# Attention value products in 64x64 TensorE tiles, with keys split over the partition halves and new instruction orders

## The chip, the cores and the metric

The kernel runs on one core of a Trainium2 chip. A core has five engines that each work through a queue of their own: TensorE (PE; its weight loads are listed as PEld), VectorE (DVE), ScalarE (ACT), GpSimd (POOL) and SyncE (SP), which here only starts transfers. Sixteen DMA engines serve them all. The metric is device time in microseconds (us).

## The reference

Windowed attention with sink keys, then a gated feed-forward network with an RMS norm in front. Four batches, eight heads, 768 positions, head size 64; window 128, four sinks; model width 512, hidden width 1536.

```python
scores = scale * np.matmul(q, k.transpose(0, 1, 3, 2))
keep = (pos[None, :] < n_sink) | ((rel >= 0) & (rel < window))      # rel = query - key
a = softmax(np.where(keep, scores, -1e9))
x = np.matmul(a, v)                          # heads side by side: 3072 x 512
xn = x / rms(x) * rms_g
g = xn @ w_gate
out = (silu(g) * (xn @ w_val)) @ w_out
```

## The kernel before

The 3072 rows are 24 blocks of 128 positions, g = 0 to 23; block g is block t = g mod 6 of batch g div 6. In the text "t=0" is a batch's first block, "last" is t=5.

For each block, q and k come from HBM as bf16 by GpSimd's queue (`load_bf16`, L351; `load_v`, L355). They are turned so that the head dimension lies on partitions: by TensorE and a copy for blocks 0 to 7 (`pe_t`, `copy_t`), by a DMA transpose on SP's queue from block 8 (`dma_t`, L457). The *scores* of a block are its 128 keys against the queries of its own and of the next block, since a window of 128 reaches from a key into the next block and no further. They are laid out with keys on partitions, so that after the exponential on ScalarE and a mask the tile e can be the stationary operand of the *value product* (`av`, L602): for each head, e of the block before (its second half) and e of the block itself, times v with a column of ones, which gives the row sums. From t=2 the four sink keys, which are then outside the window, are scored apart (`sink_s`, L739) and added to the product by one matmul for four heads (L606), u = 0 for heads 0 to 3 and u = 1 for heads 4 to 7. For nine of the blocks this sink matmul is instead issued with the next block's scores, in smaller tiles (`sink_av`, L633, "hosted").

From block 4 the scores of t=1 to 4 leave out quarters that the mask makes zero: `tri_scores` (L551) uses TensorE as four tiles of 64x64, row half by head parity, column half by key half, with matmuls of 192, 64 and 128 columns. t=0 and last blocks use 64x128 tiles (`scores` L474, `scores_last` L492), sinks 128x32. The value product uses the full 128x128 array throughout. The mask is a VectorE multiplication up to block 15 (`tri_mask` L578, `mask_dve` L542, `mask_dve_last`); from block 16 most masks are GpSimd selects (`tri_pool` L590, `mask_pool_last` L524).

VectorE then divides by the row sums (`normal`, L655), ScalarE sums the squares (`square`), VectorE works out the norm and scales (`rms`, L674), and x is transposed again (`pe_x`, `dma_x`).

The network works on six groups G of four blocks. For a hidden chunk TensorE makes g and v (L975), ScalarE the tanh (L982), VectorE two products (`silu` L986, `hidden` L993); `project` (L1004) multiplies by w_out, ScalarE evacuates, SP stores. Group 0 is done in quarters of its columns, groups 1 and 2 in halves (`CHUNKS`), so that they can begin before all four blocks are there.

Nothing decides the order while the program runs. Each piece of work is registered with `plan.op` and gets a number; `ORDER` (L70) lists the numbers for each engine, `TURNS` interleaves the engines' lists into one program order and `BANKS` names the PSUM bank that each piece takes. The nanoseconds and priorities in the `op` calls play no part in the result; only the lists do. Each engine runs its list strictly in order. Semaphores that follow from the tiles make it wait.

## Time and profile before

Three runs took 241.34, 241.84 and 242.26 us, median 241.84. The profiled execution spans 241.9 us from its first to its last instruction; the profile gives no other time for it. The granted TensorE clock is 1.00 throughout.

| stretch, us | PE busy | DVE busy | ACT busy | POOL busy |
|---|---|---|---|---|
| 30 to 62 | 31.16 of 32 | 28.37 | 21.96 | 23.49 |
| 62 to 71 | 6.89 of 9 | 8.10 | 6.58 | 3.08 |
| 71 to 100 | 28.79 of 29 | 26.84 | 15.94 | 13.61 |
| 100 to 140 | 39.69 of 40 | 36.74 | 22.55 | 9.80 |
| 140 to 180 | 39.41 of 40 | 31.70 | 20.02 | 14.65 |
| 180 to 239 | 58.66 of 59 | 33.31 | 18.01 | 0.14 |

How to read the profile: a digit in a row of slices is the busy share of one fortieth of the span, in tenths. A line of the timeline is a run of like instructions: start, length to the end of the last one, engine, line, operation, names, and the tile (rows x columns of the array) with the operand's size. The end of a matmul is modelled and takes in the drain of the array, so a following matmul starts before it; what a matmul costs is the distance to the next start. In lists of waits, "A <- B: total, times, longest" is idle time of A that ended when B did.

### The profile page before, as it was taken

Reading aid. Unit: us, or ns where it says so; the run is one execution under the profiler, and the core shown is the slowest. Engines: PE = TensorE matmul, PEld = TensorE weight load, DVE = VectorE, ACT = ScalarE, POOL = GpSimd, SP = SyncE. Lnnn points to the kernel's source line nnn. Section 1 sums busy time; section 2 is a strip of 40 time slices with the busy share of each in tenths; the row PEclk is TensorE's granted clock in tenths of the full one; section 3 lists DMA queues with packets and bytes.
Section 4 is the critical chain, followed back from the end, with each engine's and each line's share of the span. In section 5 each row is a group of like instructions: output and inputs, shape, how many; then the busy total and the mean of one; then the engine's idle time right before and its main releaser. Section 6 shows DMA issues by size and latency. Waiting matters only on the chain.

```text
span 241.9 us, 5897 instructions
## 1 busy us (share of the span) xinstructions
PE 231.3 (96%) x2329; PEld 147.6 (61%) x2354; DVE 187.4 (77%) x478; ACT 122.8 (51%) x267; POOL 89.2 (37%) x116
## 2 busy tenths in 40 slices
PE   7889999999879999999999999999999999999995
PEld 5568986876668776777876644445554444444443
DVE  3599989989979999999898989994569946537520
ACT  4776368667766574337654464454543321233112
POOL 8985894597526554000004982022540000000000
PEclk9999999999999999999999999999999999999999
DMA  9999999999999999999601999527010114101024
GB/s 128 143 183 195 182 178 194 162 143 139 137 151 152 138 143 154 132 233 156 126 2 24 119 150 123 131 70 128 3 23 0 32 36 173 43 0 47 0 87 173
DMA packets 113741, 27.42 MB, mean 113 GB/s; under 512 B 103857, under 2 KB 110769, under 8 KB 113714
## 3 DMA queue, kind: packets, MB, share of 16 engines
q0 software_dynamic: 81760, 13.90, 79.3%
q1 hardware_dynamic: 31810, 12.95, 29.8%
q8 instruction: 18, 0.29, 0.5%
q10 hardware_dynamic: 144, 0.20, 0.2%
q14 instruction: 9, 0.07, 0.1%
HBM read 28.35 MB, written 6.29 MB: 143 GB/s over the span
## 4 chain that ended last, share of the span: by engine, by line
PE 67%; DMA 20%; POOL 6%; issue 2%; DVE 2%; SPq 2%; POOLq 0%
PE v L975 20%; PE o L1008 20%; PE g L975 18%; DMA wo<-in_moe_w_out_dram 5%; DMA qkT<-q 4%; DMA wv<-in_moe_w_val_dram 4%; DMA wg<-in_moe_w_gate_dram 3%; DMA q<-in_q_dram 3%; POOL v L357 2%; SPq L459 2%; PE s L563 2%; PE av L621 2%; POOL k L353 1%; PE av L616 1%; PE o_last L1028 1%
## 5 line engine op out<-in xcount | busy, mean ns | idle before, releaser
L975 PE MATMUL v<-xnt,wv 128*128 128x128 bf16 (+2 forms) x527 | 72.2, 282 | 0.4 <-DMA wv<-in_moe_w_val_dram 0.2
L975 PE MATMUL g<-xnt,wg 128*128 128x128 bf16 (+2 forms) x521 | 71.3, 281 | 0.4
L1008 PE MATMUL o<-wo,hT 128*128 128x512 bf16 x259 | 65.3, 379 | 1.1 <-issue 0.5
L982 ACT ACTIVATE th<-g 128x512 bf16<-128x512 f32 x72 | 41.7, 599 | 48.4 <-PE g L975 48.2
L988 DVE SCALAR_TENSOR_TENSOR p<-th,g 128x512 bf16<-128x512 bf16 x72 | 48.1, 682 | 18.9 <-ACT th L982 18.7
L975 PEld LDWEIGHTS <-wv 128*128 128x128 bf16 x528 | 43.3, 98 | 21.3 <-DMA wv<-in_moe_w_val_dram 0.6
L998 DVE TENSOR_TENSOR hT<-p,v 128x512 bf16<-128x512 bf16 x72 | 48.1, 682 | 9.3 <-PE v L975 7.8
L975 PEld LDWEIGHTS <-wg 128*128 128x128 bf16 x528 | 42.8, 98 | 19.3 <-issue 1.0
L1008 PEld LDWEIGHTS <-hT 128*128 128x128 bf16 x276 | 25.4, 98 | 26.5 <-issue 0.2
L597 POOL TENSOR_SCALAR_AFFINE_SELECT e<-e 128x512 bf16<-128x512 bf16 x20 | 12.7, 656 | 54.4 <-ACT e L572 53.0
L572 ACT ACTIVATE e<-s 128x384 bf16<-128x384 f32 x52 | 23.1, 495 | 12.5 <-PE s L563 12.5
L1016 ACT ACTIVATE osb<-o 128x512 f32<-128x512 f32 x23 | 13.4, 597 | 21.8 <-PE o L1008 18.0
L357 POOL DMA_DIRECT2D v<-in_v_dram x24 | 21.3, 888 | 8.5 <-DMA q<-in_q_dram 3.8
L353 POOL DMA_DIRECT2D q<-in_q_dram x23 | 20.4, 891 | 9.9 <-DMA k<-in_k_dram 6.7
L353 POOL DMA_DIRECT2D k<-in_k_dram x23 | 20.4, 889 | 9.1 <-DMA v<-in_v_dram 4.5
L669 ACT ACTIVATE sq<-x 128x512 bf16<-128x512 bf16 x24 | 15.1, 631 | 14.8 <-DVE x L661 14.5
L661 DVE TENSOR_TENSOR x<-av,rden 128x256 bf16<-128x256 f32 x48 | 20.4, 424 | 1.7
L693 DVE SCALAR_TENSOR_TENSOR xr<-x,r,gb 128x512 bf16<-128x512 bf16 x24 | 18.7, 778 | 0.8
L621 PE MATMUL av<-v,e 128*128 128x65 bf16 x192 | 16.4, 193 | 0.3 <-DMA v<-in_v_dram 0.3
L536 ACT ACTIVATE e<-s 128x512 bf16<-128x512 f32 (+1 forms) x36 | 15.1, 519 | 1.6 <-PE s L485 1.5
L616 PE MATMUL av<-v,e 128*128 128x65 bf16 x160 | 14.8, 193 | 0.0
L621 PEld LDWEIGHTS <-e 128*128 128x128 bf16 x192 | 12.7, 97 | 2.8 <-DVE e L547 0.4
(78 smaller groups left out, 192.6 us busy)
## 6 DMA issues: line engine op xcount, KB each, us to landing
out_dram<-osb SPq DMA_DIRECT2D x23, 256.0 KB, 2.2
v<-in_v_dram POOLq DMA_DIRECT2D x24, 128.0 KB, 8.9
q<-in_q_dram POOLq DMA_DIRECT2D x23, 128.0 KB, 8.1
k<-in_k_dram POOLq DMA_DIRECT2D x23, 128.0 KB, 9.6
wo<-in_moe_w_out_dram POOLq DMA_DIRECT2D x2, 768.0 KB, 11.3
wg<-in_moe_w_gate_dram POOLq DMA_DIRECT2D x5, 256.0 KB, 8.0
wv<-in_moe_w_val_dram POOLq DMA_DIRECT2D x5, 256.0 KB, 8.9
stage<-in_k_dram SPq DMA_DIRECT2D x1, 256.0 KB, 3.0
```

The source lines that it names most:

```text
L353: nc.gpsimd.dma_start(out=T[name, g], in_=block_of(src, g))
L357: nc.gpsimd.dma_start(out=V16[b][:, t, :, 0:D], in_=block_of(v, g))
L572: nc.scalar.activation(out=e_tile(g)[:, x:x + 2, 0:TW], in_=BANK.pop(("s", g, u, hi))[:, 0:2 * TW].rearrange("p (j c) -> p j c", c=TW), fu ...
L616: nc.tensor.matmul(out=dest, lhsT=T["e", g - 1][:, x, P:2 * P], rhs=V16[b][:, t - 1, h, :], start=(t == 1), stop=False, skip_group_check=True,
L621: nc.tensor.matmul(out=dest, lhsT=T["e", g][:, x, 0:P], rhs=V16[b][:, t, h, :], start=(t == 0), stop=True, skip_group_check=True,)
L661: nc.vector.tensor_tensor(out=T["x16", g][:, 4 * u:4 * u + 4, :], in0=pvv[:, :, 0:D], in1=rden.unsqueeze(2).to_broadcast((P, 4, D)), op=AL ...
L693: nc.vector.scalar_tensor_tensor(out=T["xr", g], in0=T.pop(("x16", g)).rearrange("p h d -> p (h d)"), scalar=r[:, 3:4], in1=gb, op0=ALU.mu ...
L975: nc.tensor.matmul(out=ps[:, i * n:(i + 1) * n], lhsT=w_sb[:, kt, ft * P:(ft + 1) * P], rhs=T["xnt", G][:, kt, cols], start=(kt == 0), sto ...
L982: nc.scalar.activation(out=T["th", key], in_=BANK[("g", key)], func=ACT.Tanh, scale=0.5,)
L988: nc.vector.scalar_tensor_tensor(out=T["p1", key], in0=T.pop(("th", key)), scalar=1.0, in1=BANK.pop(("g", key)), op0=ALU.add, op1=ALU.mult,)
L998: nc.vector.tensor_tensor(out=T[hk][:, i:i + n, cols], in0=T.pop(("p1", key)).rearrange("p (n c) -> p n c", n=n), in1=BANK.pop(("v", key)) ...
L1008: nc.tensor.matmul(out=BANK[("o", G, tb)], lhsT=T["h", G, ft // 4][:, ft % 4, tb * P:(tb + 1) * P], rhs=wo[:, ft, :], start=(ft == 0), sto ...
```

## The change

From block 4 every block is "packed". Heads 0 to 3 keep their keys in partitions 0 to 63 of the score tiles and heads 4 to 7 in 64 to 127; the two halves of a block's keys lie side by side in columns. So scores and product both run as four 64x64 tiles: in the scores the row half is the head parity and the column half is u; in the product the row half is u and the column half is the half of the queries. The product issues 64x64 matmuls of 65 columns, round by round over the four tiles, and leaves out the quarters that are zero: each tile's queue has 4 or 8 matmuls for t=0, 12 or 16 for t=1 and 12 for t≥2, after the sinks, which are no longer hosted. Scores are 16 matmuls for every block. Block 4 still reads block 3's e in the old layout, so its product is partly full-array ("mixed").

For a key half that lies in the other partitions than its heads, v must move: `move_v` copies 64 partitions x 4 heads x 65 columns twice a block, on VectorE for blocks 4, 6, 7, 8, 10, 14, 15, 16, 20, 21 and 23, on ScalarE for the other nine. The mask is now one VectorE multiplication over the columns that need it (two for t=0) against a new constant `corner`, which eight VectorE instructions make; GpSimd makes no masks any more. Loads of late blocks no longer wait for scores ten blocks earlier (`LOAD_LEAD`), gates between scores and the network (`gate_of`) and the merged scores of blocks 17 and 18 are gone, and each load buffer has its own tag.

All lists are new. Read by what the numbers stand for, TensorE's list around blocks 4 to 9 (`+sa` is a hosted sink matmul, g/v/o are pieces of the network, numbered by group and place):

```
before: s4  ss  o o  pe_t k5  o  pe_x3  s5  av4  g  av4  g  pe_t q6  g  pe_t q7  o  v  av5  o  av5
        pe_t k6  v v  pe_t k7  s6  o  pe_x4  o  s7  o  pe_x5  av6  o  av6  g  o  g  av7 av7  o o v
        pe_x6  g  s8  ss  g v g  s9+sa8  v v  pe_x7  av8 av8 ...
after:  s4  ss  o o  pe_t k5  pe_t k6  o  pe_x3  AV4 s5  g  pe_t q6  pe_t q7  g g  AV5  v o v o  s6
        o  pe_x4  o o o  pe_t k7  pe_x5  v g v g  AV6 s7  v g o g  AV7 s8  o g  pe_x6  o v g
        ss  s9  v v  pe_x7  o v  AV8 AV9 ...
```

Further on, products and scores stand side by side as s11 AV10, AV11 s12, AV12 AV13, s16 AV14, AV15 AV16 s17, AV17 s18, AV18 AV19, s22 AV20, s23 AV21, AV22 AV23. GpSimd's list of loads:

```
before: ... q6  wo 0-6  k5  v4  wo 6-12  q7  v8  q8  v5  k6  k7  k8  v6  v7  q9  k9  v9  q10  k10  v10 ...
after:  ... q6  wo 0-6  k5  k6  v4  v5  q7  wo 6-12  q9  q8  q10  k8  k7  v6  v9  v7  k9  k10  q11  k11  v8 ...
```

SP's transposes begin q8, q9, k8, k9, q10, (store), q11, k10, k11 before, and q8, q10, q9, k8, k9, (store), k10, q11, k11 after; later x 8 and x 9 stand ahead of k13, and q18 ahead of x 12, x 14 and x 13.

The core of the diff (lists, bank names and removed functions left out; the removed ones are in the listing above):

```diff
+    def make_corner():
+        nc.vector.memset(corner, 1.0)
+        nc.vector.memset(corner[:, 3], 0.0)
+        for i in range(2):
+            r = slice(i * DH, (i + 1) * DH)
+            nc.vector.tensor_copy(out=corner[r, 0:3:2], in_=masks[r, 1, :, r])
+            nc.vector.tensor_copy(out=corner[r, 4:7:2], in_=masks[r, 1, :, r])
+        for i in range(2):
+            nc.vector.memset(corner[i * DH:i * DH + NS, 0:4], 1.0)
...
-            needs = [("s", g - LOAD_LEAD)] if g >= LEAD_FROM else []
+            needs = []
...
+    def width(g):
+        t = g % NT
+        return 4 * DH + TW if t == 0 else 2 * TW if t + 1 < NT else TW
+
+    def piece(g, kh):
+        t = g % NT
+        if t == 0:
+            return (kh, 4 - kh, 4 * kh)
+        return (kh, 3, 3 * kh) if t + 1 < NT else (kh, 2 - kh, 2 * kh)
...
+    def packed_scores(g):
...
+        for j in range(2):
+            for kh in range(2):
+                q0, n, c = piece(g, kh)
+                q0, n, c = t * P + q0 * DH, n * DH, c * DH
+                for u in range(2):
+                    for hi in range(2):
+                        pr, hp = slice(hi * D, (hi + 1) * D), 2 * u + j
+                        k0 = t * P + kh * DH
+                        slot, o = (("s", g, hi, j), c) if t + 1 < NT else (("s", g, hi, 0), j * w + c)
+                        nc.tensor.matmul(
+                            out=BANK[slot][u * DH:(u + 1) * DH, o:o + n],
+                            lhsT=qkT[pr, 1, hp, k0:k0 + DH], rhs=qkT[pr, 0, hp, q0:q0 + n],
+                            start=True, stop=True, tile_position=(hi * D, u * DH),
+                            skip_group_check=True,
+                        )
...
+    def packed_mask(g):
+        t, w = g % NT, width(g)
+        if t == 0:
+            for i in range(2):
+                ev = packed_e(g)[:, 2 * i * w:2 * (i + 1) * w].rearrange("p (x c) -> p x c", c=w)
+                m = corner.rearrange("p n c -> p (n c)").unsqueeze(1).to_broadcast((P, 2, w))
+                nc.vector.tensor_tensor(out=ev, in0=ev, in1=m, op=ALU.mult)
+            return
+        ev = packed_e(g).rearrange("p (x n c) -> p x n c", c=DH, n=3)[:, :, 0:3:2, :]
+        m = corner[:, 4:7:2] if t + 1 < NT else corner[:, 4:5].to_broadcast((P, 2, DH))
+        m = m.unsqueeze(1).to_broadcast((P, ev.shape[1], 2, DH))
+        nc.vector.tensor_tensor(out=ev, in0=ev, in1=m, op=ALU.mult)
+
+    def move_v(g, copy):
+        b, t = divmod(g, NT)
+        vx = T["vx", g] = vxpool.tile([P, 4, VW], BF16, name="vx")
+        for u in range(2):
+            here, there = (slice(x * DH, (x + 1) * DH) for x in (u, 1 - u))
+            copy(out=vx[here], in_=V16[b][there, t, 4 * u:4 * u + 4, :])
+
+    def packed_av(g):
...
+        queues = {}
+        for u in range(2):
+            for c in range(2):
+                own = [(0, kh) for kh in range(1 + c)]
+                old = [(1, kh) for kh in range(2) if t == 1 or kh >= c] if t and not mixed else []
+                queues[u, c] = [
+                    (j, hi, *x, x == (own + old)[0], x == (own + old)[-1])
+                    for j in range(2) for hi in range(2) for x in own + old
+                ]
+        for i in range(max(map(len, queues.values()))):
+            for (u, c), queue in queues.items():
+                if i >= len(queue):
+                    continue
+                j, hi, old, kh, first, final = queue[i]
+                k, h, rows = g - old, 2 * j + hi, slice(u * DH, (u + 1) * DH)
+                q0, n, col = piece(k, kh)
+                col = (2 * hi + j) * width(k) + (col + c + 2 * old - q0) * DH
+                vk = V16[b][rows, t - old, 4 * u + h, :] if kh == u else T["vx", k][rows, h, :]
+                nc.tensor.matmul(
+                    out=BANK["av", g, u][c * DH:(c + 1) * DH, h * VW:(h + 1) * VW],
+                    lhsT=T["e", k][rows, col:col + DH], rhs=vk, start=first and t < 2,
+                    stop=final, tile_position=(u * DH, c * DH), skip_group_check=True,
+                )
...
         if g >= PACK_FROM:
             packed_block(g)
         else:
             block_scores(g)
```

## The prediction, written before the result was known

> **What bounds the kernel now.** I read the page's busy shares and slices first, then TensorE's waits from 30 to 239 us, then single groups in the timeline.

> ```profile
> PE 231.3 (96%) x2329; PEld 147.6 (61%) x2354; DVE 187.4 (77%) x478; ACT 122.8 (51%) x267; POOL 89.2 (37%) x116
> ...
> PE   7889999999879999999999999999999999999995
> ...
> DVE  3599989989979999999898989994569946537520
> ```

> TensorE is full from slice 4 to the end; VectorE is full beside it until about 140 us. TensorE's waits from 30 us on:

> ```profile
> PE s L563 <- DMA qkT<-q: 1.3, 1, 1.3
> PE s L563 <- DMA qkT<-k: 0.8, 1, 0.8
> ...
> PE av L621 <- DMA v<-in_v_dram: 0.3, 1, 0.3
> ```

> There are three real ones: v of block 5 at 48.4 us (0.32), kT of block 8 at 64.6 us (0.78), qT of block 10 at 69 us (1.32), 2.4 us together. Everything else is work in the list's order, so a TensorE nanosecond saved or added after 30 us is one at the end, as long as no new wait opens. The chain shows where the longest wait comes from:

> ```profile
> 47.27 7.30 DMA q<-in_q_dram
> 54.59 1.20 SPq L459
> ...
> 59.75 10.61 DMA qkT<-q
> ...
> 70.49 0.54 PE s L563 x16
> ```

> A late load on POOL's queue, then SP's transposes one by one, then 10.6 us for one to land while loads crowd the DMA engines.

> **TensorE's work.** The groups to price it by (start, length, count; lengths end with the modelled drain, so I count from start to next start):

> ```profile
> 91.19 0.20 PE L616 MATMUL av<-v,e 128*128 128x65 bf16 x1
> 91.22 0.19 PE L621 MATMUL av<-v,e 128*128 128x65 bf16 x1
> 91.25 0.38 PE L1008 MATMUL o<-wo,hT 128*128 128x512 bf16 x1
> ...
> 75.38 0.54 PE L563 MATMUL s<-qkT 64*64 64x192 bf16 x24
> 75.74 0.30 PE L641 MATMUL av<-vsk,esk 64*64 64x260 bf16 x4
> 75.97 0.50 PE L975 MATMUL g<-xnt,wg 128*128 128x256 bf16 x3
> ```

> A full-array value matmul takes 0.030 us. The 24 score matmuls in 64x64 tiles carry 3,072 columns and take 0.36 us: 768 columns in each of four tiles, at the 2.4 columns per ns that 512 columns in 0.216 us give, are 0.32. So four tiles do run beside each other. Read by single starts, a group that follows one of another array shape begins 0.096 us later than the columns before it explain (0.095 to 0.099 at some 25 places, both ways): that is a **change of shape**.

> *Value product.* Before, a block with t≥1 has 16 matmuls, 16 x 0.030 = 0.48 us, and with t≥2 its sinks: two full-array ones of 0.11 where they are in the product (48.27 to 48.38), 0.135 as four tiles (75.74 to 75.97 less a change), 0.11 as two 64x128. After, a tile's queue holds 8 matmuls (t=0), 16 at most (t=1) or 12 (t≥2, the zero quarters gone). Inside a score group a 64-column matmul is followed on its own tile, with a weight load between, after 0.028 us (75.500 to 75.528). I take 0.028 for a round: 0.22, 0.45, and 12 x 0.028 + 0.135 = 0.47. Saved: six blocks with four-tile sinks (8, 9, 14, 15, 20, 21) 6 x 0.145 = 0.87; three with two-tile sinks (10, 11, 22) 0.36; four with sinks in the product (5, 16, 17, 23) 4 x 0.23 = 0.92; t=1 three times 0.03; t=0 and the mixed block 4 nothing. **2.2 us.**

> *Scores.* t=0: 2,048 columns in two tiles (0.43) become 896 per tile (0.385), three times; last blocks 0.22 become 0.17, four times; the others keep 768 per tile. **0.35 us.**

> *Changes of shape.* A product that stands alone now costs two. The new list puts most beside scores or each other (product 4 with scores 5, 6 with 7, 8 with 9, 15 with 16 and scores 17, 22 with 23). Counted through both lists from the scores of block 4, 44 changes become 55: 11 x 0.096 = **1.06 us** back.

> Net **-1.5 us**. Bounds for the new rounds: below, bare columns, 65 / 2.4 = 0.027; above, issue. A t≥2 product is 104 instructions in 0.47 us, 4.5 ns each; the densest stretch of before is 48 in 0.32 us, 6.7 ns each, but that one was bound by its columns, and its first eight instructions came in 0.012 us. At 6.7 ns a product takes 0.70. I take 0.028, the row nearest in kind.

> [...]

> **VectorE and ScalarE.** By start to next start: a mask of 1,024 columns is 0.60 (L547), the triangular one 0.66 + 0.45 = 1.11, one of 512 0.335. Blocks from 4 on before: 8 x 1.11 + 4 x 0.335 + 6 x 0.60 = 13.8, and 24 GpSimd selects (15.2 us) for the late blocks. After, all on VectorE: 13 x 0.60 + 4 x 0.335 + 3 x 1.15 (two of 896) = 12.6. New: the eleven value moves on VectorE, two copies of 64x260 each, between 0.18 (64x16) and 0.335 (128x512): I take 0.22, 4.8 us; the corner masks, eight small operations, about 1.3; one transpose copy more from ScalarE each for q and x, 0.7. VectorE +5.6 us of 180, ScalarE nine moves of about 0.7, +6. What hides it: TensorE is behind neither in its own sums. Adding durations in the order of the lists, the work that VectorE owes before each value product ends, against TensorE's sum at that product, 5.0 us early at the tightest before (blocks 6 and 7) and 4.5 to 5.0 early after (blocks 5 and 7), 8 and more from block 12 on. VectorE runs about 4.4 us further behind its sum than TensorE (block 5's last rms operation ends at 55.5 us with 42.2 summed; TensorE is at 57.9 with 49.0), so the cover early on is a few tenths. If it is gone, the excess of the first 100 us, some 2 us, comes through.

> **Loads and SP's queue.** In POOL's list q9 and q10 stand directly behind wo and v8 goes far back; v5 and k6 go ahead of q7. Loads land in order, about 1 us apart by then, so I read times off the places: v5 43.4 us (48.9 before), q9 48.9 (54.6), q10 50.5 (57.3). SP's list has q10 ahead of q9 and the k: the transposes that scores 8 and 9 wait for go out 2 to 8 us earlier. All three old waits go: **-2.4 us**. Late next: k6, whose transposition now follows k5's on TensorE with a landing near 41.5 us (0.3 to 0.5 us wait); v4 with its move ahead of product 4 (0.3); the masks of block 3, pushed back by the corner masks and a later score group (0.4). **+1.2 us.** Late loads lose their gates and the selects ahead of them (k20 went out at 133.3 us, 38 us after q20), so they crowd transposes at 100 to 120 us; those have 4 us and more in hand, so nothing there. On SP the transpose of k13 now stands behind those of x 8 and 9, and several behind the one of q18, which waits for a later load; by the same reading all are 4 to 10 us ahead of their scores. Queued behind the new waits: behind k6's transposition everything on TensorE; behind v4's move, on VectorE, a hidden product and block 4's normalisation; behind v5's move, on ScalarE, block 5's exponentials, which TensorE asks for only 3 us later.

> **Sum.** The profiled span is 241.9 us and the median 241.84, so the sum can stand on the median: 241.84 - 1.5 - 2.4 + 1.2 = **239.1 us**.

> **Rivals.**
> 1. *The tiles starve* (slower). If instructions come at 6.7 ns, a t≥2 product costs 0.23 more (13 times), t=1 0.30 and t=0 0.10 (three each): +4.2, 243.3. [...] It decides from about 0.64 us per t≥2 product. For it: 48 different weight loads in a row of 65-column matmuls occur nowhere before. Against it: the 28 ns, and eight instructions in 12 ns. Chance 0.27, of it a third for the rule.
> 2. *The cover goes* (no gain). VectorE's extra work and the pairs, which make product 8 wait for block 9's readiness, open waits of about 2.5 us beyond mine, and all is given back: 241.6. For: the few tenths of cover at 40 to 60 us. Against: the margins after. Chance 0.15.
> 3. *Forecast*, 238.2 to 240.6, chance 0.58. Its lower end is no new wait at all; its upper end, old transposes still late by a microsecond and a half.

> Less than 0.5% (1.2 us) I couldn't tell from no change here. Range 238.2 to 244.0: the forecast, rival 2 and the larger part of rival 1. Faster: 0.58 x 0.87 + 0.27 x 0.03 + 0.15 x 0.2 = 0.54; slower: 0.01 + 0.27 x 0.67 + 0.15 x 0.3 = 0.24; same 0.22.

> **What would show it.** The value product of block 9 or 16, start to next start: 0.47 right, 0.64 or more rival 1. Changes still 0.096, between 64x64 groups of scores and products none. TensorE's waits on qkT near 65 and 70 us gone; small ones at 41 to 44 us. Rival 2 would show as TensorE waiting for masks, moves or rms between 40 and 80 us. Most likely to make me wrong is a round longer than 28 ns, then a transpose that SP holds behind a later load.

## The result, and the profile after it

The changed kernel takes **244.41 us** (median of five, 243.56 to 245.23), the kernel before beside it 242.17 (241.34 to 242.59): ratio **1.0095**, 95% interval 1.007 to 1.0121. It is slower by some 2.2 us; I had forecast 239.1 us and no case of mine gave both this time and its cause. The profiled execution took 244.64 us with a span of 242.9 us.

The first lines of its page, against those shown of before:

```profile
PE 232.3 (96%) x2893; PEld 147.6 (61%) x2920; DVE 191.1 (79%) x507; ACT 127.4 (52%) x283; POOL 74.3 (31%) x92
...
PE   7899999969999999999999999999999999999995
...
DVE  2499989759999999998999989996879975543810
PEclk9799999999999999999999999999999999999999
```

TensorE has 566 weight loads more (2920 against 2354), is as busy as before, and has one slice, the ninth (48.6 to 54.6 us), in which it is idle for a third. VectorE has 3.7 us more work. (The 7 in the clock's row, a stretch at half clock from 9.3 to 12.7 us, is not of the change: e1 below has none.) What TensorE waited for from 30 us on (engine, line, waited for: us in total, times, longest):

```profile
PE v L941 <- issue: 1.8, 1, 1.8
PE o L974 <- issue: 0.8, 5, 0.2
PE v L941 <- DVE hT L964: 0.4, 1, 0.4
PE s L488 <- DVE p L954: 0.3, 1, 0.3
PE av L612 <- DVE hT L964: 0.3, 1, 0.3
```

The old waits for `qkT` (1.3 and 0.8) and for v (0.3) are gone, as forecast. (The line of `o`, 0.8 us in five places, is no wait: there the record of the first of a group's four matmuls is missing, with its 0.216 us, while all four weight loads are in the trace.) In their place stands one wait of 1.8 us for "issue", that is for nothing that the profile shows. The timeline has it in the middle of a v product (start, length, count, idle time before):

```profile
48.51 0.61 PE L941 MATMUL v<-xnt,wv 128*128 128x128 bf16 x8
50.93 0.44 PE L941 MATMUL v<-xnt,wv 128*128 128x128 bf16 x5 [1.81 <-issue]
```

The matmul that waited reads the same input as the eight ahead of it, and its weights had long landed: the last load of `wv` went out at 23.4 us, and none took more than 9.9. From the last start (48.90) to the next (50.93) are 2.03 us where 0.06 are usual: a **standstill of 1.97 us**. What the chip did meanwhile is on a DMA queue. Of all DMA queues in the window 48.0 to 49.5 us:

```profile
q0 software_dynamic: 1759, 0.22, 232.9%
q8 instruction: 1, 0.02, 4.3%
```

One packet on q8, the instruction queue: 16 KB, from 48.33 to 49.37 us, between 1,759 packets of loads. TensorE goes on 1.56 us after its end. Over the whole span the queue has 23 packets in the changed kernel and 18 in the one before:

```profile
q8 instruction: 23, 0.38, 0.6%
```

My **theory A**: TensorE's instructions come in these packets of 16 KB, a block of 256 in each. The trace's rows have 5,866 instructions of TensorE in the changed kernel and 4,736 in the one before, 255 for each of the 23 packets and 263 for each of the 18. The packet at 48.33 us started 4.0 us after the block ahead of it had been begun (44.3). By the theory a packet queues behind the loads, and TensorE stands still when 256 instructions are used up sooner than the next packet comes. Between 44.3 and 48.9 us the changed kernel uses 256 instructions in 4.6 us; the kernel before used its block from there on in 8.6 us. **Rival B**: the loss is VectorE's and ScalarE's, the cover of my rival 2, through the corner masks and the copies of v.

To tell them apart I counted TensorE's instructions up to each standstill, from the trace's rows in order: weight loads, one matmul for each of them (27 of the changed kernel's matmul records are missing) and semaphore instructions. If A holds, all stand at one remainder modulo 256, wherever the boundary is pushed, and each ends the same time after a packet.

### The profile page after: what moved, and what is told of

Same layout as the page of the kernel before. It is cut to its first block, busy times and chain, and to the rows that moved or that the text cites. A ratio compares the mean times of both kernels' runs of the same rounds, so it can differ in the third digit from the quotient of the medians.

```text
span 242.9 us, 7031 instructions
## 1 busy us (share of the span) xinstructions
PE 232.3 (96%) x2893; PEld 147.6 (61%) x2920; DVE 191.1 (79%) x507; ACT 127.4 (52%) x283; POOL 74.3 (31%) x92
## 4 chain that ended last, share of the span: by engine, by line
PE 66%; DVE 24%; issue 4%; ACT 3%; DMA 2%; SPq 0%; DVEq 0%; ACTq 0%
PE o L974 21%; PE g L941 17%; PE v L941 17%; DVE p L954 5%; DVE hT L964 5%; PE s L548 3%; DVE r L702 2%; PE av L635 2%; DVE xr L706 2%; DVE x L674 2%; DMA stage<-in_q_dram 2%; DVE vx L587 1%; PE o_last L994 1%; DVE e L580 1%; DVE e L516 1%
## 5 line engine op out<-in xcount | busy, mean ns | idle before, releaser
L941 PE MATMUL v<-xnt,wv 128*128 128x128 bf16 (+2 forms) x521 | 71.4, 281 | 2.5 <-issue 1.8
L974 PE MATMUL o<-wo,hT 128*128 128x512 bf16 x257 | 63.7, 379 | 1.7 <-issue 0.8
L954 DVE SCALAR_TENSOR_TENSOR p<-th,g 128x512 bf16<-128x512 bf16 x72 | 47.9, 683 | 13.9 <-ACT th L948 13.6
L941 PEld LDWEIGHTS <-wg 128*128 128x128 bf16 x528 | 43.4, 98 | 21.9 <-issue 0.5
L964 DVE TENSOR_TENSOR hT<-p,v 128x512 bf16<-128x512 bf16 x72 | 47.7, 683 | 10.3 <-PE v L941 7.9
L564 ACT ACTIVATE e<-s 128x384 bf16<-128x384 f32 (+1 forms) x72 | 32.1, 503 | 13.9 <-PE s L548 11.9
L706 DVE SCALAR_TENSOR_TENSOR xr<-x,r,gb 128x512 bf16<-128x512 bf16 x24 | 18.1, 752 | 0.8
L673 DVE RECIPROCAL rden<-av 128x4 f32<-128x4 f32 x48 | 8.4, 176 | 4.3 <-PE av L635 2.3
L580 DVE TENSOR_TENSOR e<-e,corner 128x1024 bf16<-128x1024 bf16 (+1 forms) x17 | 10.5, 625 | 1.5 <-ACT e L564 1.4
L635 PEld LDWEIGHTS <-e 64*64 64x64 bf16 x888 | 10.2, 106 | 1.6 <-DVE p L954 0.4
L635 PE MATMUL av<-v,e 64*64 64x65 bf16 x444 | 11.1, 193 | 0.0
L702 DVE TENSOR_SCALAR r<-r 128x1 f32<-128x1 f32 x48 | 10.0, 209 | 0.9
```

Source lines behind the costliest of these rows:

```text
L564: nc.scalar.activation(out=packed_e(g)[:, x * w:(x + n) * w], in_=BANK.pop(slot)[:, 0:n * w], func=ACT.Exp, scale=inv_sqrt_d,)
L635: nc.tensor.matmul(out=BANK["av", g, u][c * DH:(c + 1) * DH, h * VW:(h + 1) * VW], lhsT=T["e", k][rows, col:col + DH], rhs=vk, start=first ...
L706: nc.vector.scalar_tensor_tensor(out=T["xr", g], in0=T.pop(("x16", g)).rearrange("p h d -> p (h d)"), scalar=r[:, 3:4], in1=gb, op0=ALU.mu ...
L941: nc.tensor.matmul(out=ps[:, i * n:(i + 1) * n], lhsT=w_sb[:, kt, ft * P:(ft + 1) * P], rhs=T["xnt", G][:, kt, cols], start=(kt == 0), sto ...
L954: nc.vector.scalar_tensor_tensor(out=T["p1", key], in0=T.pop(("th", key)), scalar=1.0, in1=BANK.pop(("g", key)), op0=ALU.add, op1=ALU.mult,)
L964: nc.vector.tensor_tensor(out=T[hk][:, i:i + n, cols], in0=T.pop(("p1", key)).rearrange("p (n c) -> p n c", n=n), in1=BANK.pop(("v", key)) ...
```

## The experiments

All runs at once; "standstills" are those of the run's own profile between 30 and 135 us, start to next start less the usual step. The time is the median of 4 to 12 executions (e5: one), the ratio is to the kernel before on the same chip.

| run | edit to the changed kernel | standstills, us | us | ratio to before |
|---|---|---|---|---|
| after | none | 1.97 | 244.41 | 1.0095 |
| e1_same | none | 1.83 + 0.23 | 244.03 | 1.0079 (1.0055 to 1.0104) |
| e2_phase150 | 150 more warm-up instructions | 1.57 + 2.14 | 246.24 | 1.0178 (1.0155 to 1.0200) |
| e3_phase74 | 74 more | 0.39 + 1.82 + 0.26 + 0.76 | 245.49 | 1.0147 (1.0120 to 1.0174) |
| e4_corner | corner masks early | 1.76 + 0.35 | 244.26 | 1.0101 (1.0066 to 1.0137) |
| e5_before | the kernel before | none | 242.74 | |
| e6_nomove | no copies of v | 1.67 + 0.2 + 0.85 | 243.38 | 1.0058 (1.0040 to 1.0076) |
| e7_clear | 208 + 32 more | 0.88 + 0.76 | 244.20 | 1.0101 (1.0085 to 1.0117) |
| e8_clearcorner | e7 and e4 | 0.95 + 0.98 + 1.36 | 244.81 | 1.0120 (1.0103 to 1.0137) |
| e9_av5 | product 5 three pieces later | under 0.1 | 243.67 | 1.0069 (1.0050 to 1.0088) |
| e10_av5corner | e9 and e4 | 0.44 | 243.56 | 1.0058 (1.0045 to 1.0071) |
| e11_thin | pauses between loads | 1.37 | 244.60 | 1.0097 (1.0080 to 1.0114) |
| e12_beforephase | before, 150 more | none | 241.74 | 0.9977 (0.9964 to 0.9991) |
| e13_thinx | pauses, 122 more | 0.64 | 243.84 | 1.0069 (1.0042 to 1.0097) |
| e14_thinxcorner | e13 and e4 | 1.12 | 243.60 | 1.0054 (1.0032 to 1.0076) |
| e15_x122 | 122 more, no pauses | 0.48 + 3.02 + 1.50 | 249.66 | 1.0308 (1.0276 to 1.0339) |
| e16_thinxnomove | e14, no copies | 0.20 | 242.01 | 0.9997 (0.9979 to 1.0014) |
| e17_poolvx | e14, copies on GpSimd | none | 267.05 | 1.1029 (1.0996 to 1.1062) |
| e18_poolvxnopause | e17 without pauses | 2.93 + 1.09 | 248.08 | 1.0265 (1.0224 to 1.0307) |

**Shifting the boundaries (e1, e2, e3, e12).** Warm-up matmuls are cut over the same columns, in three, two or one; e3 has 0 and 37 for the two limits, e12 is the same edit to the kernel before:

```diff
-        nc.tensor.matmul(out=ps[:, 0:P], lhsT=zeros, rhs=zeros, start=True, stop=True)
+        n = 3 if i < 19 else 2 if i < 56 else 1
+        for j in range(n):
+            c = slice(j * P // n, (j + 1) * P // n)
+            nc.tensor.matmul(out=ps[:, c], lhsT=zeros, rhs=zeros[:, c], start=True, stop=True)
```

e1_same: 

> The changed kernel once more, nothing edited. Theory A (blocks of instructions): TensorE's instructions arrive in packets of 16 KB on the instruction queue, and the 1.97 us in which TensorE stands still at 48.9 us with all its data there is the wait for one such packet; it depends on the order of the instructions and not on the run, so it is here again at the same product of v, and the time is 244.4 us (243.5 to 245.2). Rival B (the cover on VectorE and ScalarE): the same 244.4 us. Rival C (the later start of the profiled run, 1.0 us at half clock, is chance): spans with that window and spans without it, some 1 us apart.

e2_phase150: 

> The same work with 75 more warm-up matmuls ahead of block 3, over the same columns (some of the warm-up matmuls are cut in two or three), so 150 more TensorE instructions: every boundary between packets of 256 instructions comes 150 instructions earlier in the work. Theory A: the packet that came too late at 48.9 us now has some 7 us instead of 4.6 us in which the block before it is used up, so the standstill of 1.97 us is gone and the time is 242.4 us (ratio to before 1.00 to 1.003). Rival B: the time of the changed kernel stays at 244.4 us, for nothing on VectorE or ScalarE changes.

e3_phase74: 

> As the run before, with 37 warm-up matmuls cut in two, so 74 more instructions. Theory A: the boundary falls where 256 instructions are used up in some 4.1 us, as bad a place as in the changed kernel or worse: a standstill of 1.9 to 2.5 us stays near 46 to 50 us, time 244.4 to 245.0 us. Rival B: 244.4 us. If both this and the run with 150 more lose the standstill, the number of instructions between boundaries is not what decides it.

e12_beforephase: 

> The kernel before, with the 75 extra warm-up matmuls (150 more instructions) of e2_phase150. Theory A: in the kernel before 256 instructions last 7 to 13 us and a packet came at least 2.8 us ahead of its need, so moving the boundaries costs nothing: ratio to before 0.999 to 1.002, no standstill that ends 1.2 to 1.8 us behind a packet. If cutting the warm-up matmuls costs by itself: the 2 us that it cost the changed kernel, ratio 1.008.

e1 shows the standstill at the same v product again, 1.83 us, and without a half-clock stretch at the start. In e2 it is gone from there, and two others come where new boundaries fall into dense places; one in the middle of a value product:

```profile
75.66 0.22 PE L638 MATMUL av<-v,e 64*64 64x65 bf16 x4
77.29 0.22 PE L638 MATMUL av<-vx,e 64*64 64x65 bf16 x2 [1.41 <-issue]
```

So e2 got slower (by 2.2 us on e1) and not faster as I had put it: I had looked at the one boundary at 49 us and not at the twenty others. The place moves as A says; the sum I had wrong. e3's worst place is at 78.7 us and not at 48, and its profiled execution also ran at half clock from 81.9 to 85.3 us (more on this at the end). In the changed kernel and all its variants but e17 there are 29 gaps of more than 0.6 us between two weight loads from 40 to 135 us. **23 of them stand at instruction 193 or 194 modulo 256, and each ends 1.2 to 1.8 us after a 16 KB packet has landed.** The other six stand elsewhere, and a named engine or the clock accounts for them. (For the 2.93 us of e18 the view names a VectorE operation, `y`, but TensorE's next weight load started before that operation ended, and it stands at 193.) e12 is the control: the cut warm-up matmuls cost the kernel before nothing. Its median is even 0.4 us under the kernel before; its profile has 2.8 us of TensorE waits after block 4's scores, where e5 has 2.9, and why it is faster stays open.

**The corner (e4, e8, e10).** The masks of the corner move up in VectorE's list, to right behind the other masks:

```diff
-... headm masks nrm0.1 ... h0 corner h0 ...
+... headm masks corner nrm0.1 ... h0 h0 ...
```

(Written with the operations' names; in the kernel these are numbers in ORDER.)

e4_corner: 

> The masks of the first block's corner (corner, 1.9 us on VectorE at 29.55 us) moved up in VectorE's list to behind the other masks at 8.4 us, where VectorE waits for the first loads. Rival B: the VectorE work that the change added decides; TensorE's waits at 34.2 us (0.49) and 37.9 us (0.24) go, and with them what followed from them, 0.7 to 1.0 us, time 243.5 us. Theory A: at most those 0.7 us at block 3, and the standstill of 1.97 us at the product of v stays; time 243.7 to 244.4 us.

TensorE's wait at block 3's scores (0.49 us in the changed kernel, VectorE's p L954 behind the corner) goes in all these runs; the 0.24 at 37 us, for block 3's masks, stays. Block 4's scores start at 38.68 us and not at 39.50. And yet the time does not fall: in e4 a second standstill of 0.35 us comes at 67 us, and over the pairs e4/e1, e8/e7, e10/e9 and e14/e13 the corner's place is worth +0.2, +0.6, -0.1 and -0.2 us. What is won at 34 us does not show in the times; e14, like e10, missed its forecast with that.

**The kernel before, once more (e5).** 

e5_before: 

> The kernel before, with a profile of its own. Theory A: its packets of instructions come with at least 2.4 us to spare everywhere, so TensorE nowhere stands still with its data there. The wait theory of the prediction (rival forecast): the three waits at 48.4 us (0.32), 64.6 us (0.78) and 69 us (1.32) are here again, within 0.2 us each. The start: block 4's scores at 38.3 us again if the 1.0 us by which the changed kernel has them later is of the change; up to 39.3 us if it is chance.

Its waits from 30 us on:

```profile
PE av L621 <- DMA v<-in_v_dram: 0.9, 1, 0.9
PE s L563 <- DMA qkT<-k: 0.9, 1, 0.9
PE o L1008 <- DVE hT L998: 0.3, 1, 0.3
```

The wait for q's transpose at 69 us is missing this time and the one for v is three times as long: these waits change from run to run, 2.0 us here and 2.4 in the first profile. No standstill. Block 4's scores start at 37.99 us (38.34 and 38.05 in the two other profiles of this kernel), so the later start of the changed kernel (38.5 to 39.5 in ten profiles without the corner edit, mean 39.1) is of the change: some 1.0 us, not the 0.4 that I had.

**The copies (e6).** The copies are dropped, and the product reads the other key half's values in their place:

```diff
-        either({"DVE": (300, lambda: move_v(g, nc.vector.tensor_copy)),
-                "ACT": (700, lambda: move_v(g, nc.scalar.copy))},
+        either({"DVE": (300, None),
+                "ACT": (700, None)},
```

e6_nomove: 

> The changed kernel without its copies of v to the other half of the partitions, on VectorE and on ScalarE: 44 pieces of work go, 4.8 us on VectorE and 4.4 us on ScalarE or nearly so. The product reads the values of the other key half in their place, so its output is not that of the reference; TensorE's instructions and their number are the same. Rival B (the cover on VectorE and ScalarE is gone and the copies decide): the waits at 62.8 us (0.50), 77.8 us (0.29) and 89.3 us (0.36) go and the time falls to that of the kernel before or under it, ratio to before 0.995 to 1.00. Theory A: the standstill of 1.8 us at 49 us stays; at most the three waits go, 0 to 0.8 us, ratio 1.005 to 1.008.

All waits for `hT` between 60 and 90 us are gone, and 0.65 us of time, while the standstills were even longer (2.7 us). B has a part, but the kernel is still slower than before (1.0040 to 1.0076).

**Clearing the standstill (e7, e9).** e7 cuts 48 warm-up matmuls in three and 8 in two, and two gate tiles by columns; e9 moves one operation (and on VectorE the division that follows it):

```diff
-... AV5 v(ft8) o2.1 v(ft4) o1.1 s6 ...
+... v(ft8) o2.1 v(ft4) AV5 o1.1 s6 ...
```

e7_clear: 

> The changed kernel with 240 more TensorE instructions over the same columns: warm-up matmuls cut in two or three (208 more instructions ahead of block 3), and the gate matmuls of tiles 4 and 0 of group 1 at 59 to 63 us cut in two halves of 128 columns (32 more). The boundaries of the packets are put where, by the lags measured in the four runs so far (a packet can be used 5.2 to 7.9 us after the block before it is used up), no block of 256 instructions is used up too early: the sum of the standstills is 0 to 0.7 us (against 1.9 in the changed kernel, 3.7 with 150 and 3.0 with 74 instructions more). Theory A: time 242.3 us, 1.2 to 1.8 us under the changed kernel, ratio to before 1.000 to 1.004. Rival B: no change, ratio 1.008. If more instructions cost by themselves, as the runs with 74 and 150 would also allow: above 245 us.

e8_clearcorner: 

> As e7_clear, and the corner masks in VectorE's list behind the other masks at 8.4 us. Theory A: the standstill for instructions is gone as in e7_clear, and with the corner out of the way TensorE's wait at 34.2 us (0.49) too: 241.6 to 242.0 us, ratio to before 0.998 to 1.001. Rival B: what moving the corner gave alone, so 244.0 us, ratio 1.008.

e9_av5: 

> The changed kernel with one piece of TensorE's list moved: block 5's value product stands three pieces later (behind the v matmuls of tile 4 of group 0, about 2.7 us), so that the 256 instructions between the boundaries at 44 and 49 us last 6.6 us and not 4.7; VectorE divides it as much later. No instruction more or less. Theory A: the standstill of 1.8 us at 49 us shrinks to 0 to 0.5 us, the marginal boundaries at 67 and 126 us stay (0 to 0.6 us together), time 242.4 to 243.0 us, ratio to before 1.001 to 1.005. Rival B (VectorE's and ScalarE's cover): VectorE gets the product later, so no better and perhaps worse, ratio 1.008 to 1.012.

e10_av5corner: 

> As e9_av5, and the corner masks early on VectorE. Theory A: another 0.5 us less (TensorE's wait at 34 us goes), if the boundary at 67 us, which cost 0.58 us in the run with the corner alone, does not take it back: 241.9 to 242.7 us, ratio 0.999 to 1.004. Rival B: ratio 1.008.

e7 and e8 failed: at the boundaries that I had chosen 256 instructions still lasted only 5.6 us at 45 us and 6.2 us at 119 us, inside the 5.2 to 7.9 us that the packets had needed in the runs before, and 1.6 and 3.3 us of standstills came at 50, 67 and 125 us. e9 did clear it; its waits have no long "issue" left, but new ones for VectorE, which now gets product 5 later:

```profile
PE o L975 <- issue: 1.0, 6, 0.2
PE s L549 <- DVE x L675: 0.5, 1, 0.5
...
PE v L942 <- DVE qkT L456: 0.3, 1, 0.3
```

From start to start there are 0.45 us too many at 47.7, 0.61 at 52.2 and 0.30 at 53.3: 1.4 of the 1.8 given back. Forecast 242.4 to 243.0, measured 243.67.

**What delays the packets (e11, e13, e15).** GpSimd sets memory ahead of each load of blocks 9 to 14 (e11) or 9 to 19 (e13), which spaces the loads; e13 and e15 add 122 warm-up instructions and differ in nothing but the pauses:

```diff
+    def pause():
+        for _ in range(7):
+            nc.gpsimd.memset(scratch, 0.0)
     def load_bf16(name, src, g):
+        if 9 <= g <= 19:
+            pause()
```

e11_thin: 

> The changed kernel with a pause of some 0.5 us (seven small memsets) on GpSimd ahead of each load of blocks 9 to 14, from 36 to 80 us, so that fewer loads stand in the DMA queues. Theory A with the packets held up by the loads: a packet starts 2 to 3 us after the block before it is used up where it took 3.9 us at 44 us and 4.9 us at 51 us, and the standstill at 49 us falls from 1.8 to 0.3 to 1.0 us; time 242.8 to 243.8 us if no load comes too late. If the packets' delay is not of the loads: 3.9 us and 1.8 us again, 244.0 us.

e13_thinx: 

> The changed kernel with both aids and no work moved: the pauses of e11 on GpSimd ahead of the loads of blocks 9 to 19, and 61 more warm-up matmuls over the same columns (122 instructions), which puts the boundaries of the packets at 43, 48 and 77 us, where by the lags of e11 no packet comes late. Theory A: standstills for instructions 0 to 0.7 us in sum (1.9 in the changed kernel); time 1.2 to 1.8 us under the changed kernel's, 242.4 to 243.0 us, ratio to before 1.001 to 1.005. If the standstill is not what the time goes by: ratio 1.008 to 1.010 as before.

e15_x122: 

> The 122 more warm-up instructions of e13 without the pauses. Theory A with the packets held up by the loads: the standstill at 49 us is gone, but with packets 3 to 5 us late some 2 to 3.5 us of standstill come at 78, 96 and 118 us; ratio 1.010 to 1.016. If the boundaries alone set it: as e13.

A pause took 1.3 us and not 0.5 (loads 2.2 us apart, with a load's own 0.87). The packets' delay below runs from the weight load with which a block of 256 begins (remainder 193 or 194) to the start of the next packet. In e11 it stayed 3.8 us at 44 us (4.0 in e1), where the pauses had hardly begun, so e11 kept 1.37 us of standstill and missed its forecast; it fell from 2.9, 4.8 and 4.3 us (at 62, 68 and 78 us in e1) to 1.2, 1.5 and 2.3. The pair e13 and e15 is the sharpest of the study, for **TensorE's list is the same in both**. The DMA engines around 70 to 79 us, first e15 (72 to 79), then e13 (70 to 77); the second line of each is the q loads' count, size and time to landing:

```profile
DMA  9999999999999999999999999999999999999999
...
q<-in_q_dram POOLq DMA_DIRECT2D x3, 128.0 KB, 9.2
```

```profile
DMA  9999999990009999912979999947997117999999
...
q<-in_q_dram POOLq DMA_DIRECT2D x2, 128.0 KB, 3.6
```

With the queues full a load lands after 9.2 us and a packet of instructions starts 4.4 to 5.0 us after the block ahead of it had been begun, between 65 and 101 us; with gaps a load lands after 3.6 us and the packets at the same boundaries start after 0.1 to 3.1 us. e15 has 5.0 us of standstills, e13 0.6, and e15 is **5.8 us slower** (249.66 against 243.84); a stretch at half clock behind the longest standstill adds some 1.7 us to them. That is A, with the loads as what delays the packets. e15's expectation had two of three places right and half the size. e13 missed its own (242.4 to 243.0): its profiled span is 1.2 us shorter than e1's and its standstills 1.4, but its ratio is 1.0069 against 1.0079, less than the intervals tell apart. e1's profiled span is 242.9 us, those of its other executions 241.1 to 242.4, those of e13 241.4 to 242.0, and what the other executions' standstills were no trace shows: the size of 2 us is that of the profiled ones. How much of the medians' loss the standstills are stays open.

**What is left (e14, e16, e17, e18).** e14 is e13 with the corner early; e16 leaves the copies out as well; e17 has them on GpSimd, each behind its load, and 130 in place of 122 instructions; e18 is e17 without pauses.

```diff
         either({"DVE": (300, lambda: move_v(g, nc.vector.tensor_copy)),
-                "ACT": (700, lambda: move_v(g, nc.scalar.copy))},
+                "ACT": (700, lambda: move_v(g, nc.scalar.copy)),
+                "POOL": (700, lambda: move_v(g, nc.gpsimd.tensor_copy))},
```

e14_thinxcorner: 

> As e13, and the corner masks early on VectorE. Theory A: 0.3 to 0.5 us less than e13, ratio 0.999 to 1.003.

e16_thinxnomove: 

> As e14, without the copies of v to the other half (the product reads the other key half's values in their place, so its output is not the reference's). Theory A: what is left of VectorE's part goes too (the waits at 63, 78 and 89 us, 0.5 to 1.1 us): 241.0 to 241.8 us, ratio 0.996 to 1.000. Rival B: it is here that the loss goes, more than 1.5 us under e14.

e17_poolvx: 

> As e14 (pauses, corner early), with all copies of v to the other half moved from VectorE and ScalarE to GpSimd, which is idle two thirds of the time, and 130 instead of 122 more warm-up instructions, so that the boundary at 124.5 us (0.6 to 1.1 us of standstill in e13 and e14) comes 8 instructions earlier. Theory C (what is left of the loss is the copies' load on VectorE and ScalarE): as e16, 241.4 to 242.2 us, ratio to before 0.997 to 1.001. If the copies cost by themselves, or if GpSimd's copies hold up its loads or VectorE: as e14, ratio 1.005, or worse.

e18_poolvxnopause: 

> As e17 without the pauses ahead of the loads. If the copies, which wait for their v and stand between the loads in GpSimd's list, hold the loads back enough by themselves: as e17. If not, the packets are 3 to 5 us late again from 60 to 120 us and standstills of 2 to 6 us come back as in e15: ratio 1.010 to 1.03.

e16 is level with the kernel before and 1.6 us under e14, which is also what B asked of this pair (more than 1.5). In their two profiles 0.9 of it is standstill that e16 happens not to have, and 0.4 lies outside the span (e14's times are 2.15 us above their spans, e16's 1.79); the copies' own waits would be the rest. So the copies are worth 0.6 us by e6 and at most 1.6 by this pair; which it is, these runs don't decide. e17 was a bad kernel for its question: GpSimd works off its list in order, the copies stood behind loads and pauses, and TensorE waited for them:

```profile
PE av L649 <- POOL vx L601: 17.5, 4, 6.3
```

A copy itself took 0.40 us there. e18 without pauses had 0.7 us of that wait left and 4.0 us of standstills: the copies do not hold the loads back enough. Whether copies on GpSimd, in a list made for them, would pay is open. **No version of the changed kernel beat the one before**; of all that ran, e12, the kernel before with more warm-up instructions, is the fastest.

## Why the prediction was wrong, step by step

The two profiled executions that compare best are e5 (before, 242.74 us) and e1 (after, 244.72). From TensorE's starts, term by term, with the missing matmul records counted as matmuls:

| term, us | before | after | change | forecast |
|---|---|---|---|---|
| up to block 4's scores | 37.99 | 39.50 | +1.51 | +0.4 |
| columns and rounds from there on | 192.8 | 191.4 | -1.4 | -2.55 |
| changes of shape | 4.13 | 5.18 | +1.05 | +1.06 |
| standstills for instructions | 0 | 2.06 | +2.06 | 0 |
| other waits | 2.9 | 1.6 | -1.3 | -1.6 |
| after the last matmul, and outside the span | 4.92 | 4.98 | +0.06 | 0 |
| sum | 242.7 | 244.7 | **+2.0** | **-2.7** |

- **The step that failed** is the first: "a TensorE nanosecond saved or added after 30 us is one at the end, as long as no new wait opens". The waits that I looked for were all waits for data. I had counted the product's instructions (104 in 0.47 us), but asked only whether the tiles can take them at 4.5 ns, not where they come from. They were taken at that rate for a product and then missing: the changed kernel used 256 instructions in 4.6 us, and the next packet ended 5.1 us after that block was begun, between the loads' 1,759 packets. In this pair that is 2.1 of the 4.7 us between forecast and result; the runs that cleared all or most of it (e9, e13) got 0.2 to 0.4 us of their median back, e9 with new waits in its place.
- **The loads without gates.** "They crowd transposes at 100 to 120 us; those have 4 us and more in hand, so nothing there." Right of the transposes. But loads close together delay the packets: in the two profiles of the kernel before a packet started 1.6 to 2.0 us after the block ahead of it had been begun, from 83 to 111 us (up to 3.7 between 53 and 83), in e1 3.2 to 4.8 us there, and e15 against e13 shows what that costs. No run puts the gates back into the changed kernel, so their own share is not shown.
- **The round**, 0.028 us forecast, is 0.029 to 0.035 in a product, 0.032 in the mean, so a t≥2 product with its sinks takes 0.475 to 0.525 us from its first start to its last, and with the last round some 0.51 to 0.56 and not 0.47. This is the term that was mis-sized. One of them between its neighbours:

```profile
120.18 0.28 PE L612 MATMUL av<-vsk,esk 64*64 64x260 bf16 x4
120.29 0.19 PE L635 MATMUL av<-v,e 64*64 64x65 bf16 x1
120.29 0.19 PE L635 MATMUL av<-vx,e 64*64 64x65 bf16 x1
...
120.65 0.20 PE L635 MATMUL av<-v,e 64*64 64x65 bf16 x2
121.01 0.81 PE L974 MATMUL o<-wo,hT 128*128 128x512 bf16 x3 [0.16 <-issue]
```

  From 120.18 to the last start, 120.655 in the raw rows, are 0.475 us. (The 0.16 behind it is again a missing first matmul of four.) The saving in columns and rounds was 1.4 and not 2.55 us, so this step is 1.15 of the 4.7. **Rival 1 is refuted**: at 6.7 ns for an instruction a product would take 0.70, and it took 0.51 to 0.56. The third of its chance that is put down to a rule rests on no run of this case; what the runs show is the round of 0.029 to 0.035 us. The rival's time, 243.3, is 1.1 us under the 244.41, and its mechanism was not the one. The tiles did starve, but of whole blocks of instructions and not from one instruction to the next.
- **Changes of shape**: 1.05, forecast 1.06; each still 0.095 to 0.099, and none between scores and products. Right.
- **The old waits** went, as forecast, and the new ones that I had put at 41 to 44 us, for k6 and v4, did not come. What came in their place was larger: 0.4 to 0.5 us at 62.8, 0.4 at 89.1, 0.25 at 77.6 us, all for VectorE. So rival 2 was there too; e6 and e16 put it at 0.6 to 1.6 us.
- **The start.** I had 0.4 for block 3's masks; they cost 0.24. The corner masks took 1.9 us in place of 1.3 and cost another 0.49 at block 3's scores, which I had not. Over all profiles the change starts block 4 1.0 us later; 0.3 of that stays unexplained.
- **The base.** I set the span of before equal to its median. e5 shows 1.7 us between time and span: the first profile was of an execution above the median. That shifted no term.

What stays open: what the standstills were in the executions without a trace, the small part outside the span (1.9 us in e1's runs, 1.7 in the kernel before's), and 0.2 to 0.6 us at 195 to 203 us in e13 to e16, which end 1.7 us after a packet but at remainder 201, and for which the view of e14, e15 and e16 names a VectorE operation.

## What to carry to other kernels

Cutting the product into small tiles multiplied its instructions (2,920 weight loads in place of 2,354). Before you believe the columns, count how long 256 instructions of the engine last in the densest stretch (4.6 us here), and set that against the delay of the packets on the instruction queue while the loads run (4.0 us to the start of the packet here, 1.0 for the packet, 1.56 from its end to the next matmul). A wait for "issue" in the middle of a group whose data are all there, 1.8 us here, was the sign; push the boundary by some instructions elsewhere (150 in e2), and if the wait moves with it, it is the instructions. And a wait removed ahead of such a stretch was no gain by itself: the corner's 0.49 us was worth +0.2, +0.6, -0.1 and -0.2 us.

## What the runs showed of the hardware that I had not expected

```profile
77.00:80.40 3.40, 0.59 (x3) 0.09 (x1) 3.12 (x14) 0.72 (x2) 1.75 (x2) 1.00 2.28 156
80.40:81.00 0.60, 0.56 (x6) 0.51 (x7) 0.60 (x1) 0.00 (x0) 0.57 (x1) 1.00 1.81 103
81.00:82.00 1.00, 1.00 (x7) 0.54 (x5) 0.07 (x1) 0.00 (x0) 1.00 (x2) 0.70 2.44 151
82.00:83.00 1.00, 1.00 (x3) 0.15 (x1) 0.00 (x0) 0.00 (x0) 0.18 (x1) 0.50 3.52 132
83.00:84.00 1.00, 1.00 (x21) 0.62 (x20) 0.00 (x0) 0.34 (x1) 0.93 (x2) 0.50 3.27 148
84.00:85.00 1.00, 1.00 (x7) 0.35 (x4) 0.00 (x0) 1.00 (x4) 1.00 (x2) 0.59 3.72 155
```

  The clock fell to half 1.0 us after TensorE had started again and stayed there for 3.41 us: 0.30 + 0.50 + 0.50 + 0.41 = 1.7 us of work lost. All five executions of e15 had a mean granted clock of 0.993 or less, those of e13 0.999 or more. From which length on a standstill is followed by this, the runs do not tell: the 1.8 us of e3 at 78.8 us were followed by it, the 1.8 us of e1 and the 2.9 us of e18 at 76.0 us were not. The clock in 40 slices of the span, first e3, then e18:

```profile
PEclk9999999999999799999999999999999999999999
```

```profile
PEclk9999999999999999999999999999999999999999
```

  In all traces a stretch at half clock that ends inside the span lasted 3.41 us or, in e17 with its waits of 3.9 to 6.6 us, two or three times as long.
- Four 64x64 tiles with a weight load for each of 48 matmuls in a row went at 0.029 to 0.035 us a round (120.29 to 120.66 us of the changed kernel), weight loads included; the 65 columns alone are 0.027 at the 512 columns in 0.216 us that a matmul of `o` shows.
